# Moving a write to another queue, shifting routing steps to other slots, and folding the last norm into a matrix

## The chip, the cores and the metric

The kernel runs on one core of a Trainium2 chip. The metric is device microseconds of one execution. The kernel before was run three times: 2882.76, 2883.17 and 2878.36 us, median 2882.76 us. The profile is of a fourth execution, of 2878.61 us; its span, from the first to the last instruction, is 2876.8 us.

## The reference

Three layers follow each other, for x of 8 x 3072 x 256 in fp32. Shapes and the first two layers in short:

```python
X = rfft(x, axis=1)                                  # layer 1: per frequency a 256x256 complex product,
Y = soft(Xr@w_r - Xi@w_i + b_r) + 1j*soft(Xr@w_i + Xi@w_r + b_i)   # soft threshold 0.01
x = irfft(Y).reshape(24576, 256)
h = maximum(x @ w_in, 0);  x = (h*h) @ w_out         # layer 2: 256 -> 2048 -> 256
logits = x @ phi                                     # layer 3: 32 slots, soft mixture of 8 experts
d = exp(logits - logits.max(0)); d /= d.sum(0) + 1e-9        # over the 24576 tokens
slot_input = d.T @ x                                 # 32 x 256
slot_out = per expert: maximum(slot_input @ w1, 0) @ w2
c = exp(logits - logits.max(1)); c /= c.sum(1) + 1e-9        # over the 32 slots
return c @ slot_out
```

## The kernel before, in words

**First stage (up to about 535 us).** Layer 1's transform, the complex product and half of the inverse transform. The change doesn't touch it.

**Main loop (about 535 to 2780 us).** The tokens come in 32 superblocks `s` of two blocks of 384 tokens. Each superblock goes through layer 2 in 8 units `q` (256 hidden columns each), so there are 256 units and one closing turn. In a unit TensorE does `u.product` for the new unit (psA and psX, L633; two results share each bank by a sum trick, so ScalarE copies psA away between products) and `prev.second` for the unit before (psO, helper `mm3`, L118 to L120). ScalarE copies, applies ReLU (`relu`, L649) and rounds to the high part `gh` (`hi`, L656, L658). VectorE adds, squares and makes the low part `gl` (`lo`, L673), which the second matmul of `mm3` (L119) multiplies. psA has a single bank: the next product into it waits for the ReLU or copy that reads it.

**Slots.** At four places of a unit stands `beside(k)`, k = 0 to 3, so that a superblock has 32 slots, slot = 4q + k. Two generators take steps there. `stage_d` is the last inverse transform of the next superblock, a step in each of slots 0 to 23: matmuls and copies in 0 to 5, then steps on ScalarE (`hi`, L438, slots 6, 9, 11, 13, 16, 19, 22) and "inverse steps" on VectorE (`lo` and `sub`, L441 and L444, slots 7, 8, 10, 12, 14, 15, 17, 18, 20, 21, 23). `route` does layer 3's first pass over a pair of superblocks, 23 steps, in slots that the table `pairs` lists: 18 in an even superblock, the rest in the odd one after it. Its VectorE steps are the maximum over tokens (L778, L779), the sum `ss` (L791), four passes of the softmax over slots (`over_slots`, L742 to L752), the sum `acc` over the tokens (L804), and `keep` (L761): VectorE copies the combining weights of 128 rows into the tile `co`, and a DMA writes them to the DRAM tensor `cd`, from which the end of the kernel reads them as `cc`. That DMA is issued by ScalarE's queue. In the last superblock (s = 31) `route` steps in every slot, for the pair before and for half of the last one.

All order is written by hand (manual schedule): each engine does its instructions in the order in which the code issues them, and an instruction that waits holds all behind it on its engine. SyncE's queue carries the loads: in an even step of two superblocks four tiles `zt`, in s = 31 the expert weights (L819, L830) into tiles that become free.

**Tail (from about 2781 us).** The last superblock's routing for its own two blocks (L943 to L978): logits, transposes of the tokens (`px_z`), the maxima of all slots merged through two small matmuls (`p_m`, `mr4`), the products `pz` of weights and tokens, the norm `p_s` (matmul with `same`, the matrix that adds the four groups of 32 rows), the scaling of `acc`, then `p_si`, which adds the groups. Then `hidden`, `turned` and `slots` (the experts), `pso`, and the output: matmuls `pf` of `cc` and `ro`, copies into `ob`, and 25 MB of writes from SyncE's queue.

Of the kernel before, what the change touches and what calls it, by code (L numbers as in the profile page):

```python
# [10 lines left out]
F32 = mybir.dt.float32  # L11
# [3 lines left out]
AF = mybir.ActivationFunctionType  # L15
ALU = mybir.AluOpType
AX = mybir.AxisListType
# [8 lines left out]
DM = 256  # L26
# [3 lines left out]
TOK = TB * N1  # L30
NQ = TOK // 128
# [73 lines left out]
def fft_moe_kernel(ctx, tc, x, w_r, w_i, b_r, b_i, moe_w_in, moe_w_out, moe2_phi, moe2_w1, moe2_w2,  # L105
                   c_f1, c_bm, c_cm, c_dm, c_st, out):
    nc = tc.nc
# [18 lines left out]
    def drain(it):  # L126
        for _ in it:
            pass
# [7 lines left out]
    cd = dram.tile([128, NBLK // 4, NQ, 128], F32, tag="cd", name="cd")  # L136

    ident = con.tile([128, 128], F32, tag="ident", name="ident")
    acc = con.tile([128, DM], F32, tag="acc", name="acc")
    nm = [con.tile([128, 1], F32, tag=f"nm{i}", name=f"nm{i}") for i in range(3)]  # L140
    ss = con.tile([128, 1], F32, tag="ss", name="ss")
    same = con.tile([128, 128], F32, tag="same", name="same")
# [31 lines left out]
    bias = [k1p.tile([128, 2, DM], F32, tag=f"bias{j}", name=f"bias{j}") for j in range(2)]  # L174
# [292 lines left out]
    with tc.manual_schedule():  # L467
# [249 lines left out]
        def put(s, q, p, copy):  # L717

            copy(xm[s][:, :, :, 128 * q:128 * q + 128].rearrange("p d a t -> p a d t"), p)
# [4 lines left out]
                nc.tensor.transpose(p[:, q, :rows], in_=v[:rows, 128 * q:128 * q + 128], identity=ident[:rows, :rows])  # L724
            return p

        def into_slots(r, gs, ee, p):
            for q in range(NQ):
                for g in gs:
                    nc.tensor.matmul(p[32 * g:32 * g + 32, :DM].rearrange("p (d t) -> p d t", d=2),  # L730
                                     lhsT=ee[:, q, 32 * g:32 * g + 32], rhs=block(r, g)[:, :, 128 * q:128 * q + 128],
                                     start=q == 0, stop=q == NQ - 1)
# [28 lines left out]
        def keep(r, g0, n, p, copy):  # L761
            co = rt.tile([128, NQ, 128], F32, tag="e", name=f"co{r}_{g0}")
            copy(co[:32 * n], p)
            nc.scalar.dma_start(out=cd[32 * g0:32 * g0 + 32 * n, r], in_=co[:32 * n])

        def route(r, n, bank):

# [73 lines left out]
        nc.sync.dma_start(same, c_st[:, 1])  # L841


        pairs = [(6, 7, 8, 10, 12, 13, 15, 17, 18, 20, 22, 23, 25, 26, 27, 28, 29, 30), (6, 8, 10, 12, 14, 16)]
        plan = set(range(25))
        side = {}
        prev = None
        for n in range(NSB * NW + 1):
            s, q = divmod(n, NW)
# [81 lines left out]
        def bank_o(t, name):  # L931
            return psO.tile([128, 512], F32, tag=f"o{t}", name=name)
# [11 lines left out]
                                                             psA.tile([128, 512], F32, tag="a", name="px_z2")))]  # L944
        nc.vector.tensor_reduce(out=bx[w], in_=pl[w, :TOK], axis=AX.X, op=ALU.max)
        nc.vector.scalar_tensor_tensor(out=nn[w], in0=bx[w], scalar=-1.0, in1=no[w], op0=ALU.mult, op1=ALU.min)
        nc.scalar.copy(lg[w], pl[w, :TOK])
        nc.scalar.activation(out=e[w], in_=pl[w, :TOK], func=AF.Exp, bias=nn[w], accum_out=se[w])
        put(NSB - 1, 0, ps[0], nc.vector.tensor_copy)
        pm = bank_o("00", "p_m")  # L950
        nc.tensor.matmul(pm[:1, :128], lhsT=nn, rhs=ident, start=True, stop=True)
        pe = turn_rows(e, 128, bank_o("10", "py_z1"))
        nc.scalar.activation(out=al[w], in_=no[w], func=AF.Exp, bias=nn[w], scale=-1.0)
        xe = mid([128, 2, NQ, 128], "xe", "z")
        nc.scalar.copy(xe[:, 1, :, w], pe[:, :, w])
        for g in range(4):
            nc.vector.tensor_reduce(out=mr4[:, g], in_=pm[:1, :128].rearrange("p (g s) -> p s g", g=4), axis=AX.X, op=ALU.min)
        put(NSB - 1, 1, ps[1], nc.vector.tensor_copy)
        put(NSB - 1, 2, ps[2], nc.scalar.copy)
        p = bank_o("01", "p_m2")  # L960
# [1 line left out]
        nc.vector.tensor_copy(nM, p[:, :1])  # L962
        nc.scalar.activation(out=cw, in_=nn, func=AF.Exp, bias=nM, scale=-1.0)
        nc.vector.scalar_tensor_tensor(out=ss[w], in0=ss[w], scalar=al[w], in1=se[w], op0=ALU.mult, op1=ALU.add)
        nc.vector.tensor_scalar(out=acc[w], in0=acc[w], scalar1=al[w], scalar2=None, op0=ALU.mult)
        pz = bank_o("11", "pz_z")
        into_slots(r, gs, xe[:, 1], pz)
        sw = small([128, 1], "sw", 0)
        nc.vector.tensor_tensor(out=sw, in0=ss, in1=cw, op=ALU.mult)
        p = bank_o("00", "p_s")  # L970
        nc.tensor.matmul(p[:, :1], lhsT=same, rhs=sw, start=True, stop=True)
        nc.vector.tensor_scalar(out=st, in0=p[:, :1], scalar1=1e-9, scalar2=None, op0=ALU.add)
        nc.vector.reciprocal(st, st)
        nc.vector.tensor_tensor(out=st, in0=st, in1=cw, op=ALU.mult)
        nc.vector.tensor_scalar(out=acc, in0=acc, scalar1=st, scalar2=None, op0=ALU.mult)
        nc.vector.scalar_tensor_tensor(out=acc[w], in0=pz[w, :DM], scalar=st[w], in1=acc[w], op0=ALU.mult, op1=ALU.add)
        pe = turn_rows(lg, 128, bank_o("10", "py_z0"))
        nc.scalar.copy(xe[:, 0, :, w], pe[:, :, w])  # L978
    mlp.close()
# [3 lines left out]
    with ExitStack() as p3, tc.manual_schedule():  # L983
# [24 lines left out]
        si = wk.tile([128, 2, 32], F32, tag="si", name="si")  # L1008
        p = tbank("p_si")
        for dh in range(2):  # L1010
            nc.tensor.matmul(p[:, 32 * dh:32 * dh + 32], lhsT=acc[:, 128 * dh:128 * dh + 128], rhs=same[:, :32],
                             start=True, stop=True)
        nc.vector.tensor_copy(si, p[:, :64].rearrange("p (a s) -> p a s", a=2))

# [14 lines left out]
        def turned(g, fh):  # L1029
            t = hsb.pop((g, fh))  # L1030
            pt = tbank(f"pth{g}_{fh}").rearrange("p (q n) -> p q n", q=4)
            for q in range(4):
                nc.tensor.transpose(pt[:, q], in_=t[:, 128 * q:128 * q + 128], identity=ident)
            nc.vector.tensor_copy(hT[:, g, 4 * fh:4 * fh + 4], pt)
# [13 lines left out]
        steps = [(g, fh) for g in range(2) for fh in range(FE // 512)]  # L1048
        for n, s in enumerate(steps):
            hidden(*s)  # L1050
            next(late, None)
            if n:
                turned(*steps[n - 1])
        drain(late)
        slots(0, 0, NX // 2)
        turned(*steps[-1])
# [77 lines left out]
```

## Time and profile before

| what | value |
|---|---|
| median of three runs (lowest, highest) | 2882.76 us (2878.36, 2883.17) |
| profiled execution, its span | 2878.61 us, 2876.8 us |
| TensorE matmul busy, weight load busy | 2806.6 us (98%), 2639.8 us (92%) |
| VectorE, ScalarE, GpSimd busy | 2149.8 us (75%), 1685.9 us (59%), 174.2 us (6%) |
| chain that ended last | PE 90%, DVE 5%, DMA 3% |

A busy TensorE in these numbers is not TensorE at its pace: the records of neighbouring matmuls overlap (0.33 us each, at starts 0.17 us apart), so a short wait shows only in part as idle time. Lost time is read from start to start. "idle before <-X" in a row is the time that the engine stood still before the instruction and the event that came last before it; where that event can't be what the instruction waits for, something between them in the queue was held.

### The profile page before, as it was taken

What the parts mean: (1) busy time and instruction counts of PE and PEld (TensorE: products, weight loads), DVE (VectorE), ACT (ScalarE), POOL (GpSimd) and SP (SyncE); (2) the same over time, 40 slices, a digit from 0 to 9 for tenths busy, and PEclk for the clock granted to TensorE, in tenths of its full rate; (3) what the DMA queues carried; (4) which work ended last, traced back from release to release, by engine and by line L of the source; (5) the groups of instructions that cost most, each with busy time, mean ns of one, the idle gap of its engine ahead of it and who ended that gap; (6) DMA issues with size and microseconds to landing.
All of it is one profiled execution on the core that took longest, in us unless ns stands there. A gap on an engine that the chain in (4) does not pass through costs nothing.

```text
span 2876.8 us, 46778 instructions
## 1 busy us (share of the span) xinstructions
PE 2806.6 (98%) x17543; PEld 2639.8 (92%) x17543; DVE 2149.8 (75%) x4458; ACT 1685.9 (59%) x3720; POOL 174.2 (6%) x236
## 2 busy tenths in 40 slices
PE   8999999899999999999999999999999999999995
PEld 5788889899999999999999999999999999999974
DVE  4899999777777777777777777777777777777764
ACT  3677775565555656565656565656565656565543
POOL 0344541000000000000000000000000000000000
PEclk9999999999999999999999999999999999999997
DMA  9888885200000000000000000000000000000169
GB/s 270 230 231 228 237 219 144 61 12 12 15 12 15 12 15 12 15 12 15 12 15 12 15 12 20 12 15 12 18 14 15 12 15 12 15 12 4 37 234 367
DMA packets 106389, 190.07 MB, mean 66 GB/s; under 512 B 14930, under 2 KB 75730, under 8 KB 103218
## 3 DMA queue, kind: packets, MB, share of 16 engines
q1 hardware_dynamic: 102946, 180.78, 21.9%
q10 hardware_dynamic: 3216, 6.29, 0.6%
q8 instruction: 138, 2.26, 0.3%
q14 instruction: 89, 0.73, 0.1%
HBM read 108.38 MB, written 78.64 MB: 65 GB/s over the span
## 4 chain that ended last, share of the span: by engine, by line
PE 90%; DVE 5%; DMA 3%; ACT 1%; issue 1%; SPq 1%; POOL 0%; DVEq 0%; ACTq 0%; POOLq 0%
PE psA L633 19%; PE psX L633 14%; PE psO L119 12%; PE psO L120 12%; PE psO L118 12%; PE psY L433 4%; PE psA L208 3%; PE psC L327 2%; PE psB L243 2%; PE px L714 1%; DVE ub L311 1%; PE psL L118 1%; PE psL L119 1%; PE psL L120 1%; DMA out_dram<-ob 1%; PE pz L730 1%
## 5 line engine op out<-in xcount | busy, mean ns | idle before, releaser
L119 PE MATMUL psO<-gl,wo 128*128 128x384 f32 x2048 | 687.4, 336 | 0.0
L120 PE MATMUL psO<-gh,wo 128*128 128x384 f32 x2048 | 684.7, 334 | 0.0
L118 PE MATMUL psO<-gh,wo 128*128 128x384 f32 x2048 | 684.6, 334 | 0.0
L673 DVE TENSOR_TENSOR gl<-g,gh 128x384 fp32r<-128x384 f32 x1024 | 557.1, 552 | 91.1 <-ACT gh L656 75.4
L119 PEld LDWEIGHTS psO<-gl,wo 128*128 128x128 f32 x2048 | 384.4, 188 | 7.3 <-DVE gl L673 7.3
L120 PEld LDWEIGHTS psO<-gh,wo 128*128 128x128 f32 x2048 | 384.5, 188 | 0.0
L118 PEld LDWEIGHTS psO<-gh,wo 128*128 128x128 f32 x2048 | 384.5, 188 | 0.0
L633 PE MATMUL psA<-yh,wia 128*128 128x384 f32 x1024 | 353.2, 345 | 12.6 <-ACT r L649 12.1
L633 PE MATMUL psA<-yh,wib 128*128 128x384 f32 x1024 | 348.1, 340 | 0.9 <-ACT V L639 0.8
L633 PE MATMUL psX<-yh,wia 128*128 128x384 f32 x1024 | 343.1, 335 | 0.0
L644 DVE TENSOR_TENSOR h<-psX,r 128x384 f32<-128x384 f32 x256 | 142.7, 557 | 249.5 <-PE psX L633 247.7
L649 ACT ACTIVATE r<-psA 128x384 f32<-128x384 f32 x256 | 126.1, 492 | 303.3 <-PE psA L633 262.4
L665 DVE SCALAR_TENSOR_TENSOR g<-h 128x384 f32<-128x384 f32 x512 | 281.8, 550 | 0.1
L639 ACT COPY r<-psA 128x384 f32<-128x384 f32 x256 | 123.3, 482 | 262.9 <-PE psA L633 262.9
L644 DVE TENSOR_TENSOR h<-psX,W 128x384 f32<-128x384 f32 x256 | 142.8, 558 | 178.5 <-ACT W L639 177.6
L656 ACT CAST gh<-g 128x384 fp32r<-128x384 f32 x512 | 263.0, 514 | 14.7 <-DVE g L665 11.9
L667 DVE TENSOR_TENSOR g<-r 128x384 f32<-128x384 f32 x512 | 260.3, 550 | 0.1
L639 ACT COPY W<-psA 128x384 f32<-128x384 f32 x256 | 123.3, 482 | 222.3 <-PE psA L633 220.7
L658 ACT ACTIVATE gh<-r 128x384 fp32r<-128x384 f32 x512 | 240.7, 518 | 8.1
L633 PEld LDWEIGHTS psA<-yh,wia 128*128 128x128 f32 x1024 | 192.7, 188 | 27.9 <-ACT r L649 16.9
L644 DVE TENSOR_TENSOR h<-psX,V 128x384 f32<-128x384 f32 x256 | 141.7, 554 | 76.0 <-PE psX L633 68.6
L633 PEld LDWEIGHTS psA<-yh,wib 128*128 128x128 f32 x1024 | 192.4, 188 | 2.1 <-ACT V L639 1.7
(214 smaller groups left out, 5339.6 us busy)
## 6 DMA issues: line engine op xcount, KB each, us to landing
bt<-ad SPq DMA_DIRECT2D x192, 128.0 KB, 4.5
zd<-sc SPq DMA_DIRECT2D x384, 64.0 KB, 2.8
zt<-zd SPq DMA_DIRECT2D x64, 384.0 KB, 3.5
xt<-in_x_dram SPq DMA_DIRECT2D x63, 384.0 KB, 4.3
ad<-sa SPq DMA_DIRECT2D x56, 384.0 KB, 4.2
out_dram<-ob SPq DMA_DIRECT2D x21, 1024.0 KB, 18.3
w<-in_moe_w_dram SPq DMA_DIRECT2D x5, 1024.0 KB, 12.3
raw<-in_moe_w_in_dram SPq DMA_DIRECT2D x16, 256.0 KB, 3.8
```

What stands on the lines that cost most here:

```text
L118: nc.tensor.matmul(o, lhsT=ah, rhs=bh, start=start, stop=False)
L119: nc.tensor.matmul(o, lhsT=ah, rhs=bl, start=False, stop=False)
L120: nc.tensor.matmul(o, lhsT=al, rhs=bh, start=False, stop=stop)
L633: nc.tensor.matmul(p, lhsT=w[:, k, l], rhs=r[:, j], start=start and n == 0, stop=n == 2, skip_group_check=True)
L639: nc.scalar.copy(t, self.a)
L644: nc.vector.tensor_tensor(out=h, in0=self.x, in1=t, op=ALU.add)
L649: nc.scalar.activation(out=t, in_=self.g[k].pop() if k in self.g else self.a, func=AF.Relu)
L656: nc.scalar.copy(h, self.g[k][0])
L658: nc.scalar.activation(out=h, in_=self.g[k][0], func=AF.Square)
L665: nc.vector.scalar_tensor_tensor(out=g, in0=t, scalar=0.0, in1=t, op0=ALU.max, op1=ALU.mult)
L667: nc.vector.tensor_tensor(out=g, in0=t, in1=t, op=ALU.mult)
L673: nc.vector.tensor_tensor(out=l, in0=g, in1=f(h), op=ALU.subtract)
```

## The change

1. `keep` issues its DMA from SyncE's queue and no longer from ScalarE's (17 times in a run).
2. The table `pairs` has other slots for `route`. In the new table each of its steps on VectorE stands in a slot in which `stage_d` has none on VectorE.
3. In the tail: the copy `lg` of the last logits moves behind the weights; four small reductions become one over a broadcast view; the norm's matmul `p_s` comes after two thirds of `pz`'s matmuls; and `acc` is no longer scaled by the norm: the factor goes into a copy `mean` of the adding matrix (128 x 32), which `p_si` multiplies. `acc` of the last 64 rows takes `al` and `pz` in one instruction.
4. In the experts' loop the softmax steps of the last block come after `turned` and not ahead of it.

```diff
-        def into_slots(r, gs, ee, p):
-            for q in range(NQ):
+        def into_slots(r, gs, ee, p, qs=range(NQ)):
+            for q in qs:
...
-            nc.scalar.dma_start(out=cd[32 * g0:32 * g0 + 32 * n, r], in_=co[:32 * n])
+            nc.sync.dma_start(out=cd[32 * g0:32 * g0 + 32 * n, r], in_=co[:32 * n])
...
-        pairs = [(6, 7, 8, 10, 12, 13, 15, 17, 18, 20, 22, 23, 25, 26, 27, 28, 29, 30), (6, 8, 10, 12, 14, 16)]
+        pairs = [(6, 7, 9, 10, 12, 14, 15, 17, 18, 20, 21, 23, 24, 25, 26, 27, 28, 29), (9, 11, 12, 13, 19, 22)]
...
-        nc.scalar.copy(lg[w], pl[w, :TOK])
         nc.scalar.activation(out=e[w], in_=pl[w, :TOK], func=AF.Exp, bias=nn[w], accum_out=se[w])
+        nc.scalar.activation(out=al[w], in_=no[w], func=AF.Exp, bias=nn[w], scale=-1.0)
...
-        nc.scalar.activation(out=al[w], in_=no[w], func=AF.Exp, bias=nn[w], scale=-1.0)
...
-        for g in range(4):
-            nc.vector.tensor_reduce(out=mr4[:, g], in_=pm[:1, :128].rearrange("p (g s) -> p s g", g=4), axis=AX.X, op=ALU.min)
+        nc.vector.tensor_reduce(out=mr4, in_=pm[:1, :128].rearrange("p (g s) -> p s g", g=4).unsqueeze(1).broadcast_to(
+            [1, 4, 32, 4]), axis=AX.X, op=ALU.min)
...
-        nc.vector.tensor_scalar(out=acc[w], in0=acc[w], scalar1=al[w], scalar2=None, op0=ALU.mult)
-        pz = bank_o("11", "pz_z")
-        into_slots(r, gs, xe[:, 1], pz)
         sw = small([128, 1], "sw", 0)
         nc.vector.tensor_tensor(out=sw, in0=ss, in1=cw, op=ALU.mult)
+        pz = bank_o("11", "pz_z")
+        into_slots(r, gs, xe[:, 1], pz, range(2))
         p = bank_o("00", "p_s")
         nc.tensor.matmul(p[:, :1], lhsT=same, rhs=sw, start=True, stop=True)
+        into_slots(r, gs, xe[:, 1], pz, range(2, NQ))
...
-        nc.vector.tensor_tensor(out=st, in0=st, in1=cw, op=ALU.mult)
-        nc.vector.tensor_scalar(out=acc, in0=acc, scalar1=st, scalar2=None, op0=ALU.mult)
-        nc.vector.scalar_tensor_tensor(out=acc[w], in0=pz[w, :DM], scalar=st[w], in1=acc[w], op0=ALU.mult, op1=ALU.add)
+
+        mean = rt.tile([128, 32], F32, tag="mean", name="mean")
+        nc.vector.tensor_scalar(out=mean, in0=same[:, :32], scalar1=st, scalar2=cw, op0=ALU.mult, op1=ALU.mult)
+        nc.vector.scalar_tensor_tensor(out=acc[w], in0=acc[w], scalar=al[w], in1=pz[w, :DM], op0=ALU.mult, op1=ALU.add)
+        nc.scalar.copy(lg[w], pl[w, :TOK])
...
-            nc.tensor.matmul(p[:, 32 * dh:32 * dh + 32], lhsT=acc[:, 128 * dh:128 * dh + 128], rhs=same[:, :32],
+            nc.tensor.matmul(p[:, 32 * dh:32 * dh + 32], lhsT=acc[:, 128 * dh:128 * dh + 128], rhs=mean,
...
-            next(late, None)
             if n:
                 turned(*steps[n - 1])
+            next(late, None)
```

How the instructions stand on their engines, at three places. First ScalarE in unit 3 of superblock 3, before; `W_3` is the copy of psA, `r_3_1` the ReLU of the same unit, `r_4` the next unit's copy:

```order
L639 COPY W_3_9916<-psA_3_9860 128x384
L764 DMA cd<-co_0_9931 128x384
L649 ACTIVATE r_3_1_9937<-psA_3_9860 128x384
L656 CAST gh_3_3_9939<-g_3_3_9928 128x384
L639 COPY r_4_9960<-psA_4_9955 128x384
```

The same place now:

```order
L639 COPY W_3_9916<-psA_3_9843 128x384
L649 ACTIVATE r_3_1_9934<-psA_3_9843 128x384
L656 CAST gh_3_3_9936<-g_3_3_9928 128x384
L639 COPY r_4_9957<-psA_4_9952 128x384
L649 ACTIVATE r_3_2_9970<-h_3_2_9941 128x384
```

The DMA is gone from between the copy and the ReLU; it stands in SyncE's queue now, behind the loads of `zt` for superblock 5 and ahead of those for superblock 6.

Second, VectorE in unit 2 of superblock 3, before; L444 and L441 are inverse steps, L751 and L752 a routing step:

```order
L665 SCALAR_TENSOR_TENSOR g_2_0_9778<-h_2_0_9760 128x384
L444 TENSOR_TENSOR yf_0_9565<-yf_2_9567,yf_0_9565 128x384
L751 RECIPROCAL sm_9472<-sm_9472 128x12
L752 TENSOR_TENSOR xe_9418<-xe_9418,sm_9472 128x384
L673 TENSOR_TENSOR gl_1_2_9791<-g_1_2_9772,gh_1_2_9770 128x384
L673 TENSOR_TENSOR gl_2_0_9801<-g_2_0_9778,gh_2_0_9799 128x384
L644 TENSOR_TENSOR h_2_3_9809<-psX_2_9751,W_2_9807 128x384
```

The same unit now:

```order
L665 SCALAR_TENSOR_TENSOR g_2_0_9776<-h_2_0_9758 128x384
L444 TENSOR_TENSOR yf_0_9565<-yf_2_9567,yf_0_9565 128x384
L673 TENSOR_TENSOR gl_1_2_9787<-g_1_2_9770,gh_1_2_9768 128x384
L673 TENSOR_TENSOR gl_2_0_9797<-g_2_0_9776,gh_2_0_9795 128x384
L748 TENSOR_REDUCE sm_9442<-xe_9401 128x12
L749 TENSOR_SCALAR sm_9442<-sm_9442 128x12
L644 TENSOR_TENSOR h_2_3_9807<-psX_2_9749,W_2_9805 128x384
```

Slot 8 (k = 0) has lost its routing step, and the step of slot 9 (k = 1) stands behind the two `gl`; the reciprocal and L752 now close the unit, in slot 11.

Third, VectorE in the tail, from the norm's `sw` on, before:

```order
L965 TENSOR_SCALAR acc<-acc,alz 64x256
L969 TENSOR_TENSOR sw_33038<-ss,cw 128x1
L972 TENSOR_SCALAR st<-p_s 128x1
L973 RECIPROCAL st<-st 128x1
L974 TENSOR_TENSOR st<-st,cw 128x1
L975 TENSOR_SCALAR acc<-acc,st 128x256
L976 SCALAR_TENSOR_TENSOR acc<-pz_z,st,acc 64x256
L1013 COPY si<-p_si 128x64
```

and now:

```order
L965 TENSOR_TENSOR sw_33026<-ss,cw 128x1
L971 TENSOR_SCALAR st<-p_s 128x1
L972 RECIPROCAL st<-st 128x1
L975 TENSOR_SCALAR mean<-same,st,cw 128x32
L976 SCALAR_TENSOR_TENSOR acc<-acc,alz,pz_z 64x256
L1014 COPY si<-p_si 128x64
```

Two scalings of `acc` and one of `st` are gone; one of 128 x 32 has come.

## Rows read from the trace of the kernel before

**Rows 1.** Chain of waits, main loop: start, duration (us), what.

```profile
2774.80 0.52 PE psA L633 x3
```

**Rows 2.** Windows: length, busy of PE, PEld, DVE, ACT, POOL, then PEclk, DMA share, GB/s.

```profile
548.00:2776.00 2228.00, 2215.08 (x13567) 2163.77 (x13567) 1637.66 (x3377) 1313.34 (x2896) 0.00 (x0) 1.00 0.06 17
```

**Rows 3.** Waits, whole execution: who waited for whom: us, times, longest.

```profile
PE psA L633 <- ACT r L649: 12.1, 14, 0.9
...
PEld psO L119 <- DVE gl L673: 7.3, 29, 0.3
...
PE psA L633 <- ACT V L639: 0.8, 2, 0.5
```

**Rows 4.** Timeline of ScalarE, superblock 29, slot 14: start, us, instruction, idle before.

```profile
2601.90 0.33 ACTq L764 DMA_DIRECT2D cd<-co  x1
2602.32 0.49 ACT L649 ACTIVATE r<-psA 128x384 f32<-128x384 f32 x1 [2.92 <-DVE h L644]
```

**Rows 5.** Timeline of VectorE, the same slot.

```profile
2601.31 0.55 DVE L763 COPY co<-pc 128x384 f32<-128x384 f32 x1
```

**Rows 6.** Timeline of TensorE, the same stretch.

```profile
2601.67 0.34 PE L120 MATMUL psO<-gh,wo 128*128 128x384 f32 x1
2602.87 0.45 PE L633 MATMUL psA<-yh,wia 128*128 128x384 f32 x1 [0.86 <-ACT r L649]
2603.15 0.34 PE L633 MATMUL psA<-yl,wia 128*128 128x384 f32 x1
```

**Rows 7.** Timeline of VectorE, superblock 29, slot 8: the routing step.

```profile
2587.98 0.56 DVE L752 TENSOR_TENSOR xe<-xe,sm 128x384 f32<-128x384 f32 x1
```

**Rows 8.** Timeline of TensorE just after it.

```profile
2588.75 0.34 PE L118 MATMUL psO<-gh,wo 128*128 128x384 f32 x1
2589.06 0.44 PE L119 MATMUL psO<-gl,wo 128*128 128x384 f32 x1
2589.33 0.34 PE L120 MATMUL psO<-gh,wo 128*128 128x384 f32 x1
```

**Rows 9.** Timeline of TensorE, superblock 28, just after slot 8.

```profile
2519.44 0.44 PE L119 MATMUL psO<-gl,wo 128*128 128x384 f32 x1
2519.72 0.34 PE L120 MATMUL psO<-gh,wo 128*128 128x384 f32 x1
```

**Rows 10.** Timeline of VectorE: superblock 28 behind slot 13, superblock 29 behind slot 19.

```profile
2528.77 0.56 DVE L644 TENSOR_TENSOR h<-psX,W 128x384 f32<-128x384 f32 x1 [0.72 <-ACT W L639]
...
2612.11 0.56 DVE L644 TENSOR_TENSOR h<-psX,r 128x384 f32<-128x384 f32 x1 [0.82 <-PE psX L633]
```

**Rows 11.** Timeline of all engines in the tail.

```profile
2782.60 0.56 DVE L945 TENSOR_REDUCE bxz<-pl_z 64x1 f32<-64x384 f32 x1
...
2784.37 0.87 DVE L957 TENSOR_REDUCE mr<-p_m 1x32 f32<-1x128 f32 x4 [0.29 <-PE p_m L951]
...
2785.60 1.49 PE L730 MATMUL pz_z<-xm,xe_z 128*32 128x256 f32 x12
...
2787.02 0.38 PE L971 MATMUL p_s<-sw,same 128*128 128x1 f32 x2
...
2787.83 0.16 DVE L974 TENSOR_TENSOR st<-st,cw 128x1 f32<-128x1 f32 x1
...
2788.42 0.49 DVE L976 SCALAR_TENSOR_TENSOR acc<-pz_z,st,acc 64x256 f32<-64x256 f32 x1
```

**Rows 12.** Timeline of TensorE, the experts' first matmuls.

```profile
2789.96 1.94 PE L1023 MATMUL ph<-ea,si 128*32 128x512 f32 x8 [0.36 <-issue]
...
2793.34 1.05 PE L1023 MATMUL ph<-ea,si 128*32 128x512 f32 x8
...
2795.18 0.66 PE L1033 MATMUL pth<-ident,hsb 128*128 128x128 f32 x4
```

**Rows 13.** Windows of the experts' first matmuls and of the output stage.

```profile
2788.00:2792.00 4.00, 2.68 (x16) 1.21 (x20) 1.78 (x5) 0.15 (x1) 0.00 (x0) 0.74 1.10 350
2813.00:2876.00 63.00, 35.55 (x352) 24.65 (x352) 28.88 (x48) 24.80 (x47) 0.00 (x0) 0.72 0.97 401
```

## The prediction

> **What bounds the kernel now.** I read the page first: TensorE is busy for 98% of the span and makes 90% of the chain that ended last. So a change is worth only what it takes out of TensorE's own sequence, or out of the few places where TensorE stands still. The chain of waits in the main loop gives the pace: three matmuls of 128x384 in 0.52 us, 0.17 us from start to start [rows 1]. The windows give the clock: granted 1.00, which is 2.4 GHz, over the whole of the main loop, and 2215.1 of 2228 us busy [rows 2]. That leaves 12.9 us of plain idle time, but records overlap, so the loss is larger than that and has to be read from starts.
>
> The waits say where TensorE stands: 14 times for a ReLU of psA on ScalarE (12.1 us), 2 times for the copy V on ScalarE (0.8 us), and 29 times for a low part `gl` of VectorE (7.3 us of the weight load) [rows 3]. I then looked for what these places have in common, in the timelines. The 14 lie one in each odd superblock from 3 to 29, in slot 14, where `keep` stands; the 2 lie in superblock 31, again at a `keep`. The 29 lie just after slot 8, in the 14 odd superblocks and in the 15 even ones from 2 to 30.
>
> At a `keep` the reader should see the following. VectorE's copy `co` ends at 2601.86 [rows 5]; 0.04 us later ScalarE's queue issues the DMA of `co`, and the ReLU starts behind it, after 2.92 us of standing still [rows 4]. The row names VectorE's `h` as the releaser, but this ReLU reads psA and no `h`: it was held by the DMA ahead of it, which waited for `co`. TensorE's next product goes into the same bank and waits for the ReLU: 2602.87 instead of 2601.84 [rows 6].
>
> **The write moved to SyncE.** TensorE's start to start at a `keep` is 2602.87 - 2601.67 = 1.20 us where the pace is 0.17: 1.03 lost. The matmul behind it comes after 0.28 us and not 0.17: another 0.11 [rows 6]. 14 x 1.14 = 16.0 us. For the two in superblock 31 I take the idle time, 0.8 us in all [rows 3], and for each the same difference between idle and lost that the 14 show (1.14 - 0.86 = 0.28): 0.8 + 0.56 = 1.4 us. Nothing else holds ScalarE there: without the DMA the ReLU waits for its own matmuls only. The upper bound is the whole 17.4 us. The lower bound would be that the ReLU is late for another reason; then at least the DMA's own issue, 0.33 us [rows 4], leaves ScalarE, which is 59% busy, and TensorE gains nothing.
>
> On SyncE the DMA now waits for `co`, and what is queued behind it waits too: in the loop the loads of `zt` for a later superblock, which are issued once per superblock and moved 17 GB/s in a stretch with a DMA share of 0.06 [rows 2]; in superblock 31 weight loads that are used only in the tail. I cost that wait at nothing. The cover is long: such a tile is first read more than a superblock later.
>
> Here the Trainium skill speaks against the change: the page "DMA: Bandwidth & Descriptors", section "Issuing engines are not separate DMA queues", says that DMAs of all issuing engines run on the same 16 DMA engines and that spreading them saves only the sequencer's time to start one, usually small. By that rule the 17 moves would be worth 17 times an issue on an engine with time to spare, so nothing. The trace agrees on the issue, 0.33 us [rows 4], and shows what the rule leaves out: the time for which the issuing engine's queue stands until the data is there.
>
> **The routing steps.** In an odd superblock two routing instructions of VectorE come between the inverse step of slot 8 and the two `gl`; the larger ends at 2588.54 [rows 7], and TensorE's matmul with `gl` starts 0.31 us after its neighbour, the next 0.27 after that [rows 8]: 0.14 + 0.10 = 0.24 lost, times 14 = 3.4 us. In an even superblock the same place shows 0.28 for the matmul behind the one that waited [rows 9]: 0.11, times 15 = 1.7 us. In the new table neither slot 8 has a routing step, so I take both to zero: 5.0 us.
>
> What the new slots cost: each step has to fit into the idle time of VectorE at its new place. Steps with k = 1 (slot 9 in both parities, slot 13) stand ahead of the sum with W, which today waits 0.72 us for ScalarE's copy (the first of [rows 10]). Steps with k = 3 (slot 11, and `keep` in slot 19) stand at a unit's end, ahead of a sum that waits 0.82 us for TensorE (the second of [rows 10]). A step is one pass of 128x384, 0.55 to 0.56 us [rows 5, 7], with at most one instruction of a few elements at 0.16 [rows 11]: 0.55 to 0.72 us. So they fit, with 0 to 0.3 us to spare, and where they don't it is by hundredths, and TensorE needs the `gl` behind them only later. The bounds: nothing lost, or at worst a wait of the size of today's (0.24 us) at one new place in each superblock, which gives the 5.0 us back. I take nothing lost, since no other wait of TensorE for VectorE stands in the list today, although inverse steps and `gl` meet in every superblock. ScalarE's and TensorE's share of `route` moves by a slot or two and keeps its count; TensorE's extra matmuls cost the same in any slot.
>
> **The tail.** Three terms. The four reductions take 0.87 us; one pass over 384 elements from PSUM takes 0.56 [rows 11], so 512 would take 0.75 by length (estimate): 0.12 saved, between 0 and 0.3. The norm's matmul starts 1.42 us after the first of 12 passes of `pz` [rows 11]; with 8 ahead of it, it starts 4/12 of that earlier, 0.47 us, since its operand `sw` also loses a scaling of `acc` ahead of it. The last passes of `pz` then run beside the reciprocal. Of VectorE's chain, two steps go from `st` times `cw` at 2787.83 to the sum at 2788.42 [rows 11], 0.59 us, and `mean` comes, 128x32: 0.16 (as the one-column step) to 0.35; I take 0.2, nearest to the small one, so 0.39 saved. Sum 1.0 us, between 0.4 and 1.3. The experts' loop only swaps steps of VectorE which waits there for TensorE: nothing. The output stage moves 401 GB/s with a DMA share of 0.97 [rows 13]: its length is set by the writes, and what comes earlier ahead of it ends earlier by as much. The last `keep` is now ahead of the last `cc` load and of the output writes in one queue; they waited for its landing before as well, so nothing.
>
> **The sum.** 17.4 + 5.0 + 1.0 = 23.4 us. The profiled execution took 2878.6 us with a span of 2876.8, so 1.8 us lie around it: 2855.2 us on its own footing. That execution and the lowest run agree; the median of the three, 2882.76, is 4.2 us above, and a median of new runs may lie at either level: 2855.2 or 2859.4. I forecast the middle, 2857 us.
>
> **Rivals.**
> - *The lateness of VectorE moves along.* `keep` stalls go, but the new places cost as much as slot 8 did: 5.0 us back, 2862. For it: 0.72 us of room and up to 0.72 of work. Against it: a late sum there isn't at once a late matmul. 0.13.
> - *The clock stays up in the tail.* The first 16 passes of the experts took 3.38 us (2789.96 to 2793.34), the next 16 1.84 [rows 12]; in that stretch the granted clock was 0.74 on average [rows 13], so partly at the lower level, 1.2 GHz. Before it TensorE had stood still around the norm. With that shorter, the fall may not come: 1.5 us more, 2855.5. 0.13. The page "TensorE: Matmul & The Clock Gate", section "Part 1: The HAM clock gate", says that activity is what lifts the lower clock; the trace agrees as far as the fall follows the emptier stretch.
> - *Only the issue is saved,* because the ReLU is late for another reason than the DMA: 17.4 us stay, 2874. Rows 4 speak against it. This is also what the skill's rule on issuing engines would give. 0.03.
> - *Slower: VectorE overflows in the odd superblocks.* `keep` in slot 19 stands among the inverse steps of slots 14 to 23. If its work there exceeds the 0.82 us that are free, VectorE is late for the next unit, ScalarE after it, and the loss runs on through slot 23. To be slower than before by 0.2% it would have to lose (23.4 + 5.8) / 14 = 2.1 us in each odd superblock, nearly twice what a `keep` costs today; it decides from 0.82 us on, and the copy records 0.55. 2889 then; 0.03.
>
> **How the numbers follow.** The forecast has 0.65, with 2853 to 2861 as its own range; 0.03 is left for what no case here holds. With the cases beside it the range is 2851 (clock case, lower level of the runs, a little more in the tail) to 2864 (VectorE's case, upper level). A difference under 0.2%, 5.8 us, can't be told from none here. Faster by more than that: forecast, clock case, VectorE's case and most of the issue case, 0.95; within 0.2%: 0.02; slower: 0.03.
>
> **What the profile after would show.** Right: odd superblocks shorter by about 1.4 us each and even ones by 0.1 to 0.2; no wait of `psA` for the ReLU of 0.9 us, the 29 waits for `gl` gone; `cd<-co` in SyncE's queue; `p_si` about 1 us sooner after `pl_z`. Wrong: a wait of `psA` for ScalarE at the same or another slot, waits for `gl` after slots 9, 11, 13 or 19, or a tail in which the first output write is held by the last `cc`.

## The result, and the profile after

The changed kernel took 2857.61 us (median of four runs, 2856.75 to 2858.44) against 2881.76 us of the kernel before in the same comparison (four runs, 2878.36 to 2883.17): a ratio of 0.9918, 95% interval 0.9901 to 0.9935. The forecast was 2857, its range 2851 to 2864. The profiled execution took 2858.44 us with a span of 2856.7 us.

The windows over the main loop, of the kernel after (columns as in [rows 2]):

```profile
551.00:2755.00 2204.00, 2204.00 (x13564) 2165.13 (x13563) 1638.30 (x3376) 1313.84 (x2894) 0.00 (x0) 1.00 0.06 17
```

The 12.9 us of idle time of [rows 2] are gone to the last hundredth: 2204.00 busy of 2204.00. The list of waits says the same. Of the lines of [rows 3] neither the 14 and 2 of psA nor the 29 of `gl` are there any more. What is left for these banks stood in the list of before too: 16 waits of a weight load of psA that name no engine (10.0 us in both), and a few short ones, 0.9 us at most; the last two of these three lines show such, all in the loop's first superblock:

```profile
PE pso L1064 <- DMA cst<-in_c_st_dram: 2.3, 1, 2.3
...
PE psA L633 <- ACT W L639: 0.6, 1, 0.6
...
PEld psX L633 <- DVE h L644: 0.5, 2, 0.3
```

The first of these three lines is new, and it lies in the tail; it comes back below.

The same slot as in [rows 4 to 6], superblock 29, slot 14. ScalarE after:

```profile
2582.89 0.49 ACT L649 ACTIVATE r<-psA 128x384 f32<-128x384 f32 x1 [1.14 <-PE psA L633]
```

TensorE after:

```profile
2584.03 0.33 PE L120 MATMUL psO<-gh,wo 128*128 128x384 f32 x1
2584.20 0.33 PE L633 MATMUL psA<-yh,wia 128*128 128x384 f32 x1
2584.37 0.33 PE L633 MATMUL psA<-yl,wia 128*128 128x384 f32 x1
```

The ReLU waits for its own matmuls and nothing else (1.14 us where [rows 4] has 2.92), and it is done 0.8 us before TensorE wants the bank. TensorE goes on at 0.17 us per start, where [rows 6] has 1.20 and 0.28.

`keep` now stands at the end of unit 4 (slot 19). VectorE there, after:

```profile
2591.94 0.55 DVE L673 TENSOR_TENSOR gl<-g,gh 128x384 fp32r<-128x384 f32 x1
2592.40 0.55 DVE L763 COPY co<-pc 128x384 f32<-128x384 f32 x1
2593.31 0.56 DVE L644 TENSOR_TENSOR h<-psX,r 128x384 f32<-128x384 f32 x1 [0.36 <-PE psX L633]
```

The copy took 0.46 us (from its neighbour's start to its own) out of the 0.82 us of [rows 10]; 0.36 us are left, so nothing behind it is late.

The beginnings of superblocks 28, 29 and 30, each marked by ScalarE's first copy `r` of psA, with the first and the last such copy of the loop, before:

```profile
537.35 0.48 ACT L639 COPY r<-psA 128x384 f32<-128x384 f32 x1 [0.28 <-PE psA L633]
...
2494.39 0.48 ACT L639 COPY r<-psA 128x384 f32<-128x384 f32 x1 [1.08 <-PE psA L633]
...
2565.56 0.48 ACT L639 COPY r<-psA 128x384 f32<-128x384 f32 x1 [1.09 <-PE psA L633]
...
2634.92 0.48 ACT L639 COPY r<-psA 128x384 f32<-128x384 f32 x1 [1.08 <-PE psA L633]
...
2769.63 0.48 ACT L639 COPY r<-psA 128x384 f32<-128x384 f32 x1 [1.11 <-PE psA L633]
```

and after:

```profile
539.90 0.48 ACT L639 COPY r<-psA 128x384 f32<-128x384 f32 x1 [0.33 <-PE psA L633]
...
2477.13 0.48 ACT L639 COPY r<-psA 128x384 f32<-128x384 f32 x1 [1.08 <-PE psA L633]
...
2548.14 0.48 ACT L639 COPY r<-psA 128x384 f32<-128x384 f32 x1 [1.08 <-PE psA L633]
...
2616.11 0.48 ACT L639 COPY r<-psA 128x384 f32<-128x384 f32 x1 [1.08 <-PE psA L633]
...
2749.26 0.48 ACT L639 COPY r<-psA 128x384 f32<-128x384 f32 x1 [1.08 <-PE psA L633]
```

An even superblock takes 71.01 us (before 71.17), an odd one 67.97 (before 69.36). From the first of these copies to the last, the loop takes 2209.36 us and took 2232.29: 22.93 us shorter.

The span is only 20.1 us shorter. Two things took the other 2.8 us. The loop began 2.56 us later (539.90 instead of 537.35 us) behind a first stage that the change doesn't touch; in the nine other kernels profiled below, whose first stage is the same, it began between 538.0 and 542.2 us, so this is scatter. And the tail, which had become faster ahead of the output, gave all of that back and 0.2 us more. The tail after, all engines:

```profile
2762.23 0.56 DVE L945 TENSOR_REDUCE bxz<-pl_z 64x1 f32<-64x384 f32 x1
...
2764.00 0.68 DVE L955 TENSOR_REDUCE mr<-p_m 1x128 f32<-1x512 f32 x1 [0.29 <-PE p_m L951]
...
2766.03 0.38 PE L969 MATMUL p_s<-sw,same 128*128 128x1 f32 x2
...
2766.84 0.30 DVE L975 TENSOR_SCALAR mean<-same,st,cw 128x32 f32<-128x32 f32 x1
2767.18 0.49 DVE L976 SCALAR_TENSOR_TENSOR acc<-acc,alz,pz_z 64x256 f32<-64x256 f32 x1
...
2768.71 1.07 PE L1024 MATMUL ph<-ea,si 128*32 128x512 f32 x8 [0.36 <-issue]
...
2772.29 0.66 PE L1034 MATMUL pth<-ident,hsb 128*128 128x128 f32 x4
...
2781.25 0.33 SPq L1004 DMA_DIRECT2D cst<-in_c_st_dram  x1
...
2786.25 0.37 ACT L1045 COPY so<-p2o 128x256 f32<-128x256 f32 x1 [3.67 <-PE p2o L1042]
2788.52 1.10 PE L1064 MATMUL pso<-so,cst 128*128 128x256 f32 x4 [2.34 <-DMA cst<-in_c_st_dram]
2788.66 0.32 SPq L1060 DMA_DIRECT2D cc<-cd  x1
...
2792.63 1.02 SPq L1100 DMA_DIRECT2D out_dram<-ob  x2
```

Counted from L945, with [rows 11, 12] beside it: `p_s` starts after 3.80 us (before 4.42), the sum L976 after 4.95 (5.82), the experts' first matmul after 6.48 (7.36), their first `pth` after 10.06 (12.58). So the chain gave 0.87 us, and between `ph` and `pth` another 1.64 us came by itself. The first of these windows of the kernel after goes with it:

```profile
2767.00:2771.00 4.00, 3.36 (x31) 1.68 (x35) 1.21 (x4) 0.56 (x2) 0.00 (x0) 1.00 1.07 353
...
2790.00:2792.60 2.60, 2.46 (x28) 2.18 (x32) 0.87 (x4) 0.74 (x3) 0.00 (x0) 0.62 0.38 135
...
2792.60:2856.60 64.00, 36.70 (x364) 25.42 (x356) 29.33 (x48) 25.06 (x48) 0.00 (x0) 0.69 0.95 394
```

The granted clock stayed at 1.00 where [rows 13] have 0.74; which of the tail's edits kept it there no run tells apart. Then `so` is ready at 2786.62, but `pso` starts only at 2788.52: it reads the 128 KB tile `cst`, whose load SyncE issued at 2781.25 behind five of the experts' weights `w` and seven loads of `cc`, and which landed 7.1 us later. The issue itself had waited 2.7 us for a `w` to land, which `cst` doesn't read (the experiment with only the tail shows why):

```profile
SPq L1004 <- DMA w<-in_moe_w_dram: 2.7, 1, 2.7
```

The chain that ended last, after, in order of time:

```profile
2768.46 12.78 DMA w<-in_moe_w_dram
2781.25 7.13 DMA cst<-in_c_st_dram
```

TensorE stood still there, the granted clock fell behind it (0.62 on average in the second window, so partly at the lower level, 1.2 GHz), and the first output write started 30.40 us after L945, where it had started after 30.16 (2812.76 before). The output then took 64.0 us in both.

### The profile page after: what moved, and what is told of

Read it like the earlier page. It is cut to its first block, busy times and chain, and to the rows that moved or that the text cites. A ratio compares the mean times of both kernels' runs of the same rounds, so it can differ in the third digit from the quotient of the medians.

```text
span 2856.7 us, 46821 instructions
## 1 busy us (share of the span) xinstructions
PE 2802.2 (98%) x17543; PEld 2647.9 (93%) x17543; DVE 2150.7 (75%) x4453; ACT 1687.2 (59%) x3720; POOL 174.4 (6%) x236
## 4 chain that ended last, share of the span: by engine, by line
PE 92%; DMA 3%; DVE 3%; SPq 0%; ACT 0%; issue 0%; POOL 0%; DVEq 0%; ACTq 0%; POOLq 0%
PE psA L633 19%; PE psX L633 14%; PE psO L120 12%; PE psO L118 12%; PE psO L119 12%; PE psY L433 4%; PE psA L208 3%; PE psC L327 2%; PE psB L243 2%; PE px L714 1%; PE psL L118 1%; PE psL L119 1%; PE psL L120 1%; DMA out_dram<-ob 1%; DVE ub L311 1%; PE pz L730 1%
## 5 line engine op out<-in xcount | busy, mean ns | idle before, releaser
L639 ACT COPY V<-psA 128x384 f32<-128x384 f32 x256 | 123.0, 480 | 141.1 <-PE psA L633 141.1
```

Of the source, the lines that this page charges most:

```text
L639: nc.scalar.copy(t, self.a)
```

## The experiments

Each kernel was read in two ways: by its time, and by stretches of its own trace, which scatter far less than the times. "Loop" is from the first to the last copy `r`; "first write" is the first output write counted from `pl_z`, the first matmul of the tail, 1.63 us ahead of L945 in the traces of before and after; "stage" is from the first write to the end, all in us. A ratio is to the runs of before in the same comparison. The single time of a kernel with one run says little, since the runs of before lie between 2876 and 2885 us; such a kernel is read from its trace.

| kernel | us, median | ratio to before (95%) | loop | first write | stage |
|---|---|---|---|---|---|
| before | 2881.76 | 1 | 2232.3 | 31.79 | 64.0 |
| after | 2857.61 | 0.9918 (0.9901, 0.9935) | 2209.4 | 32.03 | 64.0 |
| only the queue | 2864.97 | 0.9947 (0.9930, 0.9964) | 2217.0 | 31.66 | 64.0 |
| only the slots | 2861.23 | 0.9929 (0.9914, 0.9944) | 2211.8 | 31.84 | 64.0 |
| only the tail | 2883.30, one run | | 2232.3 | 34.63 | 64.1 |
| after, cst first, new layout | 2856.72 | 0.9917 (0.9902, 0.9932) | 2209.1 | 29.64 | 65.5 |
| after, cst first, same layout | 2856.61 | 0.9910 (0.9894, 0.9927) | 2209.0 | 29.26 | 65.2 |
| after, slot 8 used again | 2858.61, one run | | 2211.4 | 32.03 | 64.0 |
| after, keep as before | 2879.45, one run | | 2226.7 | 35.23 | 64.1 |
| cst first, no edit of the tail | 2857.36, one run | | 2208.9 | 31.84 | 64.2 |
| cst first, last keep early | 2853.96 | 0.9906 (0.9890, 0.9923) | 2209.0 | 29.29 | 64.2 |

**Only the queue** (kernel before, one line).

```diff
-            nc.scalar.dma_start(out=cd[32 * g0:32 * g0 + 32 * n, r], in_=co[:32 * n])
+            nc.sync.dma_start(out=cd[32 * g0:32 * g0 + 32 * n, r], in_=co[:32 * n])
```

> Only the write of the weights moved to SyncE, slots and tail as before. Theory (the queue's wait and the collisions in slot 8 are two losses that add): odd superblocks 69.36 -> 68.22 us, even ones stay at 71.18, the main loop 17.4 us shorter, the waits for gl stay at 29, time 0.6% shorter. Rival (the waits for gl came from the same lateness): the waits for gl go too, odd 67.97, even 71.01.

The loop became 15.3 us shorter: 1.0 us in each odd superblock (68.35), nothing in the even ones (71.18), and 1.4 us in superblock 31, less 0.35 us by which the loop's first superblock was longer; that one scatters by up to 0.4 us between kernels. The 16 waits of psA for ScalarE are gone; the 29 for `gl` stand there with the same 7.3 us as in [rows 3], and a line that had 2 waits before has 16:

```profile
PEld psX L633 <- DVE h L644: 2.9, 16, 0.3
```

14 of these stand in slot 14 of the odd superblocks, 0.17 us each. So 0.13 us of each stall stayed as a smaller wait, 1.8 us in all (68.35 where 68.22 was expected): in slot 14 the copy `co` still stands inside a unit, and VectorE is late for `h` behind it. The rival, that the waits for `gl` go too, is out.

**Only the slots** (kernel before, the new table, `keep` still on ScalarE).

```diff
-        pairs = [(6, 7, 8, 10, 12, 13, 15, 17, 18, 20, 22, 23, 25, 26, 27, 28, 29, 30), (6, 8, 10, 12, 14, 16)]
+        pairs = [(6, 7, 9, 10, 12, 14, 15, 17, 18, 20, 21, 23, 24, 25, 26, 27, 28, 29), (9, 11, 12, 13, 19, 22)]
```

> Only the new slots, the write still on ScalarE's queue. Theory (wherever the write stands on ScalarE it holds TensorE by about 1.1 us): only the waits for gl go, odd superblocks 69.36 -> 69.12, even 71.18 -> 71.01, 5.0 us in all. Rival (the place decides, not the queue: in slot 19, at a unit's end, ScalarE is held before a copy of psA that TensorE needs only 12 matmuls later, 2.1 us): ScalarE's copy is about 0.6 us late, TensorE doesn't wait, odd superblocks 67.97 as in the changed kernel, some 21 us in all; only the two stalls of superblock 31, 1.4 us, stay.

The loop became 20.5 us shorter, four times what I had given the table; the rival of the expectation came near (it said some 21). It takes out the 29 waits for `gl` and also the 14 of `keep`, with the DMA still on ScalarE. ScalarE of this kernel in superblock 29, slot 19:

```profile
2594.60 0.33 ACTq L764 DMA_DIRECT2D cd<-co  x1
2594.97 0.48 ACT L639 COPY r<-psA 128x384 f32<-128x384 f32 x1 [1.25 <-PE psX L633]
```

At a unit's end the next instruction of ScalarE is a copy of psA that has to wait for TensorE anyway (0.62 us at this place in the kernel after). The DMA makes it 0.6 us late (1.25 against 0.62 us of waiting), and TensorE's next product into psA comes only after it has ended; odd superblocks take 68.07 us, 0.1 more than in the kernel after. What the table can't help is superblock 31, where `route` steps in every slot: its two stalls stay, 1.39 us in the starts.

**Keep as before in the new table** (slot 14, ScalarE).

```diff
-            nc.sync.dma_start(out=cd[32 * g0:32 * g0 + 32 * n, r], in_=co[:32 * n])
+            nc.scalar.dma_start(out=cd[32 * g0:32 * g0 + 32 * n, r], in_=co[:32 * n])
...
-        pairs = [..., (9, 11, 12, 13, 19, 22)]
+        pairs = [..., (9, 11, 12, 13, 14, 22)]
```

> The changed kernel with keep of the odd superblocks back in slot 14 and its DMA back on ScalarE's queue, all other steps in their new slots. Theory (the DMA in ScalarE's queue waits for co, and the ReLU behind it is late, where a keep stands inside a unit): TensorE stands 1.03 + 0.11 us once in each odd superblock again, 14 waits of psA for ScalarE, odd superblocks of 69.1 us, loop 16 us longer. Rival (the stall of 1.1 us came from VectorE being late with co in the old crowded table, and in the new table co comes in time): less than half of it comes back, odd superblocks below 68.5 us.

The loop is 17.4 us longer than after: 16.1 us in the odd superblocks (69.11), as expected, and 1.45 us in superblock 31, whose two stalls are back too and which the expectation had not counted; 0.2 us is scatter of the first superblock. The stall is back in full, though slot 8 is free. ScalarE, superblock 29, slot 14, and VectorE's copy:

```profile
2599.43 0.33 ACTq L764 DMA_DIRECT2D cd<-co  x1
2599.86 0.49 ACT L649 ACTIVATE r<-psA 128x384 f32<-128x384 f32 x1 [2.92 <-DVE h L644]
...
2598.85 0.55 DVE L763 COPY co<-pc 128x384 f32<-128x384 f32 x1
```

These are [rows 4] again, with the same 2.92 us, and `co` ends 0.03 us ahead of the DMA (2598.85 + 0.55), where it was 0.04. The cause of the 17.4 us is this: a DMA in a compute engine's queue that waits for its data, where the work behind it is wanted at once. Either cure (another queue, or a place where the engine waits anyway) takes most of it: the queue alone 15.6 of the 17.4 us (14.2 in the odd superblocks, 1.4 in superblock 31), the place alone all but 0.1 us in each odd superblock and the 1.4 us of superblock 31.

**Slot 8 used again.**

```diff
-        pairs = [..., (9, 11, 12, 13, 19, 22)]
+        pairs = [..., (8, 11, 12, 13, 19, 22)]
```

> The changed kernel with one routing step of the odd superblocks put back from slot 9 to slot 8 (keep stays on SyncE in slot 19). Theory (collision with gl): the waits of TensorE for gl come back in the 14 odd superblocks, 0.17 to 0.24 us each, so odd superblocks of 68.14 to 68.21 us instead of 67.97, a loop longer by 2.4 to 3.4 us; even ones unchanged. Rival (what matters is only how many slots without an inverse step are used, since the step in slot 8 has the same room as slot 9): odd superblocks stay at 67.97 and the loop changes by less than 0.5 us.

Odd superblocks take 68.15 us instead of 67.97: 0.18 us, 14 times, with 14 waits for `gl` in the list again. TensorE of this kernel, superblock 29 just after slot 8:

```profile
2571.34 0.34 PE L118 MATMUL psO<-gh,wo 128*128 128x384 f32 x1
2571.58 0.44 PE L119 MATMUL psO<-gl,wo 128*128 128x384 f32 x1
2571.86 0.34 PE L120 MATMUL psO<-gh,wo 128*128 128x384 f32 x1
```

0.24 and 0.28 us between starts where 0.17 is the pace: [rows 8] in small. One step in this slot is enough, a pass of 0.55 us and a small instruction of 0.17; the rival, that any slot without an inverse step has room, is out.

**Only the tail** (kernel before with parts 3 and 4 of the change).

> Only the edits of the tail and of the experts' loop. Theory (what the tail gains is lost again where pso waits for the load of its constant, which stands behind 7.75 MB in SyncE's queue): main loop as before, p_si 0.9 us sooner after pl_z, the second pair of expert matmuls sooner by up to 2.5, pso not sooner, the end within 0.4 us of before, counted from pl_z. Rival (the tail's gain counts, and the late pso of the changed kernel came with the write on SyncE): pso and the end 0.9 to 2.5 us sooner after pl_z.

The loop is as before. Up to `pth` it gains what the kernel after gains (11.68 us from `pl_z`, before 14.21), and it ends 2.9 us later than before, counted from `pl_z`. The theory had the place of the wait right and its size wrong (the end was to stay within 0.4 us of before); the rival is out. SyncE's queue of this kernel, and the wait of the issue at L1004:

```profile
2793.66 9.37 SPq L1002 DMA_DIRECT2D cc<-cd  x7
2809.81 0.33 SPq L1004 DMA_DIRECT2D cst<-in_c_st_dram  x1
...
SPq L1004 <- DMA cd<-co: 6.8, 1, 6.8
```

`cst` went out 6.8 us after the seventh `cc`, `pso` waited 3.6 us for it, and the clock was 0.59 in the 4 us around `pso`. The kernel with `keep` as before in the new table did the same (`cst` 27.6 us after `pl_z`, `pso` 4.2 us late). Both have the tail's edits and the last `keep` on ScalarE, and in both the list of waits names the landing of the last `keep`'s write for that issue. The traces hold the reason: they record for each DMA the semaphore that its landing sets and the one that its issue waits for. In the tail the DMAs of both queues take eight semaphores in turn, and an issue waits until the DMA that had its semaphore last has landed. In these two kernels `cst` has the semaphore of the last `keep`'s write; in the kernel after it has that of the last `w` (the 2.7 us there), in the kernel before that of the first `cc` (0.6 us). Why the program gives them out in another order in these kernels stays open.

**The load of cst first** (kernel after; first with the tile laid out ahead of the weights, then with all tiles in their old places).

```diff
+        cst = wk.tile([128, 2, 128], F32, tag="cst", name="cst")
+        nc.sync.dma_start(cst, c_st[:, 2:4])
         for e in range(e0, NE):
...
-        cst = wk.tile([128, 2, 128], F32, tag="cst", name="cst")
-        nc.sync.dma_start(cst, c_st[:, 2:4])
```

> The changed kernel with the load of the constant cst issued ahead of the five loads of w, nothing else changed. Theory: pso starts right behind the experts' last matmul, 2.3 us sooner than in the changed kernel, and the end comes as much sooner after pl_z; time about 0.1% under the changed kernel. Rival (the amount of data ahead of the output decides, not this one load): pso is sooner, but the first output write or the end stays where it is.

> The changed kernel with one load moved: cst (128 KB) goes to SyncE's queue ahead of the 7.75 MB of expert weights, the tiles keep their places in memory. With cst first and the tiles laid out anew, the output writes began 2.4 us sooner than in the changed kernel, but from the first write to the end 65.5 us passed instead of 64.0. Theory A: the longer output stage came from the new places of the tiles. Then here the first write again begins about 2.4 us sooner, the stage takes 64.0 us again, and the run ends 2.4 us below the changed kernel (about 2855.2). Theory B: writes that begin sooner do not end sooner by as much, because something else of the stage (the last keep's landing, the last cc) holds it: the stage takes 65 us or more again and the end comes at most 1 us sooner (2856.7).

(The 7.75 MB named there are 5 MB of weights and 2.7 MB of `cc`.) In both `pso` no longer waits for `cst`, and the first write came sooner, by 2.4 and 2.8 us; in both the output stage took longer, 65.5 and 65.2 us, so that the end came 0.9 and 1.6 us sooner from `pl_z`. So the end doesn't come as much sooner as `pso` does, as the first theory had it. The layout was not the reason for the longer stage, so theory A is out; theory B had the stage right and its end, at most 1 us sooner, 0.6 us short. The windows around the first write with the same layout:

```profile
2788.00:2791.80 3.80, 3.28 (x40) 2.14 (x36) 1.27 (x4) 1.18 (x5) 0.00 (x0) 1.00 0.25 97
2791.80:2857.00 65.20, 38.48 (x352) 26.35 (x352) 29.18 (x48) 24.99 (x48) 0.00 (x0) 0.66 0.95 393
```

The stage moves bytes at nearly the rate of the kernel after (393 against 394 GB/s). 65.2 us at 393 are 25.6 MB, 64.0 at 394 are 25.2: 0.4 MB more, which is the size of the last `cc` load (384 KB) and worth 1.0 of the 1.2 us. It goes out only when the last `keep`'s write has landed (28.65 us from `pl_z`), 0.6 us ahead of the first write, and ahead of it the DMA engines are three quarters idle.

**cst first, without the tail's edits.**

> The kernel before with keep on SyncE, the new table of slots and cst ahead of the expert weights with the tiles in their old places; the norm, the reductions and the experts' order stay as before. It differs from the changed kernel with cst first (same places) only by the tail's edits. Theory (the tail's edits are worth what they gave ahead of the experts once cst is out of the way): the experts' end and the first output write come 0.9 us (the chain to p_si) to 2.5 us (with the clock that stayed up) later after pl_z than there, and the end with them. Rival (the tail is held by the last keep or the weights' landing): the first output write and the end differ by less than 0.3 us.

From `pl_z`, `p_si` starts at 7.99 us (with the edits 7.11), `pth` at 14.26 (11.68), the first write at 31.84 (29.26), and the end is at 96.04 (94.47). The theory was right on the first write, 2.6 us later; the end is only 1.6 us later and not as late as the write, and the rival is out. So the edits are worth 2.6 us ahead of the outputs and 1.6 at the end, once `cst` is out of the way; and `cst` first without them is worth nothing. The clock case is seen here side by side, though not which of the tail's edits makes it. The window of the experts' first matmuls without the edits:

```profile
2767.50:2771.50 4.00, 3.60 (x24) 1.67 (x28) 0.94 (x3) 0.00 (x0) 0.00 (x0) 0.72 1.08 363
```

and with them:

```profile
2770.50:2774.50 4.00, 3.88 (x35) 1.44 (x36) 0.37 (x2) 0.78 (x2) 0.00 (x0) 1.00 1.09 368
```

**cst first and the last keep early.**

```diff
-        for b in range(NB - 1):
+        for b in range(4):
             nc.sync.dma_start(cc[b], cd[:, 2 * b:2 * b + 2])
...
         slots(0, 0, NX // 2)
+        keep(r, 2, 2, turn_back(r, 2, 2, xe[:, 0], tbank("pc_z")), nc.vector.tensor_copy)
+        for b in range(4, NB - 1):
+            nc.sync.dma_start(cc[b], cd[:, 2 * b:2 * b + 2])
         turned(*steps[-1])
         slots(0, NX // 2, NX)
-        keep(r, 2, 2, turn_back(r, 2, 2, xe[:, 0], tbank("pc_z")), nc.vector.tensor_copy)
```

> The changed kernel with cst first (tiles in their old places), and the tail's last keep moved ahead by half of the experts' second product, its write ahead of the last three of the first seven loads of cc. In the run with cst first and nothing else, the first output write began 29.26 us after pl_z, the write of the last keep had landed only at 28.65, the last cc load (384 KB) went out 0.6 us ahead of the outputs, and from the first output write to the end 65.2 us passed where the kernels whose last cc went out 1.7 to 4.0 us ahead take 64.0 to 64.2. Theory (the last cc load's 384 KB, about 0.9 us at 420 GB/s, fell into the output stage because the write of keep queued behind the cc loads): the last cc goes out at least 2 us ahead of the first output write, the stage takes 64.0 to 64.3 us again, the first write stays at 29.3 after pl_z, and the end comes about 1 us sooner than there (93.4 instead of 94.5 after pl_z; 2855.4 as a median if the rest stays). Rival (writes that begin sooner run beside something else, so that the stage is longer whatever the last cc does): the stage takes 65 us or more, the end stays at 94.5.

SyncE's queue of this kernel:

```profile
2779.36 0.45 SPq L764 DMA_DIRECT2D cd<-co  x1
2779.87 1.55 SPq L1059 DMA_DIRECT2D cc<-cd  x3
2785.21 0.32 SPq L1062 DMA_DIRECT2D cc<-cd  x1
2788.37 1.86 SPq L1102 DMA_DIRECT2D out_dram<-ob  x2
```

The last `cc` goes out 3.2 us ahead of the first write, the stage takes 64.2 us again, and the end is 93.53 us after `pl_z`, where 93.4 was expected. The rival, a stage of 65 us or more, is out. Its four runs (2852.37 to 2855.77) lie below the four of the changed kernel (2856.75 to 2858.44), though each was timed beside its own runs of before, and the intervals of the two ratios overlap. Its median is the lowest here; against `cst` first alone (2851.05 to 2858.78) only the traces show the gain, 0.9 us.

## Why the prediction was right, point by point

**The loop's sum: right.** 22.4 us were expected of it, 22.93 came. Odd superblocks are 1.39 us shorter (1.4 expected), 19.4 us in all, even ones 0.17 (0.1 to 0.2), 2.5 us in all, and superblock 31 gave 1.39 (1.4); the first superblock was 0.4 us longer.

**The write moved to SyncE: size and cause right, the share not.** Putting `keep` back costs 16.1 us in the odd superblocks and 1.45 in superblock 31, where the sum had 16.0 and 1.4. But I gave it all to the queue and only 5.0 us to the table, as if the two added up. Alone they give 15.3 and 20.5 us; the queue on top of the table gives 2.4. The failed step is the sentence on the slots that counted only slot 8: the move of `keep` to slot 19 is a cure of its own for the same stall. The sum came out because it held the whole of the stalls and the two cures together took all of them, not because the shares were right. The wait put on the loads of `zt` at nothing was right: no engine waits for them in the loop of the kernel after (the traces show two of them in each superblock, not four in every second one).

**Only the issue saved** (2874): refuted. ScalarE's queue lost 0.33 us per issue, and TensorE got back 1.15 us per odd superblock, as putting the DMA back shows. The rule in the Trainium skill's page "DMA: Bandwidth & Descriptors", section "Issuing engines are not separate DMA queues", that spreading DMAs over issuing engines saves only the time to start one, would also have given this rival. Here the moved write took the wait for the data off ScalarE's queue, and that alone was worth 15.3 us.

**The routing steps: right.** Slot 8 was the place, and the new places have room: 0.36 us left of the 0.82 at slot 19. The term was read short in the even superblocks: it took 0.11 us each from the second matmul of [rows 9] and left out the first, which starts 0.23 us after its neighbour, 0.06 late; 0.17 x 15 = 2.5 us came where 1.7 stood. With 3.3 us of the odd ones that is 5.9 us for 5.0. The neighbour, in the trace of before:

```profile
2519.21 0.34 PE L118 MATMUL psO<-gh,wo 128*128 128x384 f32 x1
```

The rivals in which VectorE's lateness moves along, or overflows, are out: no wait for `gl` is left.

**The chain in the tail: right in size, wrong in worth.** Expected 0.12 + 0.47 + 0.39 = 0.98 us; measured 0.19 for the reduction (0.87 to 0.68), 0.43 for `p_s` beyond that, 0.25 for VectorE's chain, where `mean` took 0.30 and not 0.2; 0.87 in all. The step that failed is "what comes earlier ahead of it ends earlier by as much". It took the length of the output stage for all that holds it, and did not ask when `cst`, the last operand ahead of it, would land. In the kernel before `cst` went out 6.6 us ahead of `pso` and was no wait; with `pso` ready 2.5 us sooner it became one. The tail's net worth was -0.2 us, not 1.0.

**The clock's rival (0.13): it came true,** 1.64 us against 1.5, and is not seen in the time, since the same wait swallowed it.

**The last keep at nothing: right here by cover alone.** Its write and the last `cc` were hidden behind the wait for `cst`; with that gone they cost 1.0 us (65.2 to 64.2). That they would cost nothing held by luck.

On its own footing the forecast was 2855.2, and the profiled execution took 2858.4: 2.6 us of scatter ahead of the loop and 1.2 us of tail, less 0.5 us that the loop gave beyond its sum. I had put the forecast 1.8 us above that footing for the scatter of the runs. That it landed 0.6 us from the median is luck in part: the allowance, which stood for the scatter, also covered the tail's miss.

## What to carry to other kernels

A DMA that waits for its data holds the engine that issues it; before moving it to another queue, look whether there is a place in the same queue where the engine waits anyway, since each of the two may be most of the cure. When edits touch one stall, work out each of them alone and the second on top of the first. And before counting a gain ahead of a stage, list every operand that this stage still waits for, with the time at which its load lands: a load queued last behind megabytes is the next wait.

## What the runs showed of the hardware that I had not expected

- A load of 128 KB queued behind 5 MB of weights and 2.7 MB of `cc` landed 7.1 us after its issue, though it was needed ahead of the `cc`. Issued ahead of all of them it cost nothing that the first write shows (31.84 us from `pl_z` without the tail's edits, as in only the slots).
- A DMA's issue can wait for a landing that its data has nothing to do with, by a shared semaphore: 2.7 us for `cst` in the kernel after, 6.8 us in only the tail.
- After TensorE stood still for 2.3 us at `pso`, the granted clock was 0.62 on average over the 2.6 us ahead of the first output write; in the kernels in which it did not wait there it stayed at 1.00 in that stretch.
- One reduction over 512 elements of PSUM on one partition took 0.68 us, less than the 0.75 that its length had suggested from a pass over 384 (0.56).
- The output stage moved 391 to 397 GB/s in all eleven kernels. One late load of 0.4 MB made it about 1.0 us longer; the spread of the rate is worth as much, and what sets it isn't known.
- The start of the loop scattered over 4.8 us (537.3 to 542.2) between kernels with the same first stage, more than most of the terms here. Inside the loop superblocks agreed to hundredths between kernels with the same edits there; the loop as a whole, with its first superblock, to 0.5 us.
